# Two first blocks turned into token order in PSUM, constants and memory loads first, and value sums moved inside a unit

## The chip, the cores and the metric

The kernel runs on one core of a Trainium2 chip. Its five engines run their own instruction queues side by side: TensorE (PE, with PEld for its weight loads), VectorE (DVE), ScalarE (ACT), GpSimd (POOL) and SyncE (SP). SP, ACT and POOL also issue DMAs. The metric is the device time of one execution in microseconds, as the median of several runs. What the profile shows comes from one execution.

## The reference

A chunked attention with a memory, followed by a gated feed-forward layer. There are 4 sequences of 768 tokens with 8 heads of 64. Chunks are 32 tokens; each chunk sees 16 tokens to its left, 8 to its right and 8 memory rows of its sequence. The feed-forward layer takes the 3,072 tokens with 512 features each.

```python
for c in range(S // 32):
    l_start, r_end = max(0, 32 * c - 16), min(S, 32 * c + 32 + 8)
    k_full = concatenate([mem_k, k[:, :, l_start:r_end]], axis=2)
    v_full = concatenate([mem_v, v[:, :, l_start:r_end]], axis=2)
    scores = q[:, :, 32 * c:32 * c + 32] @ k_full.T / sqrt(64)
    a = exp(scores - max(scores)); a = a / sum(a)
    out[:, :, 32 * c:32 * c + 32] = a @ v_full
x = out.transpose(0, 2, 1, 3).reshape(3072, 512)
result = (maximum(x @ w_gate, 0) * (x @ w_val)) @ w_out
```

## The kernel before

The tokens are worked in 8 blocks (n = 0 to 7) of 384, two for each sequence. A block has 4 windows of 96 queries; a window's keys are 120 tokens and the 8 memory rows, which is 128 partitions. Heads are taken in 4 pairs (hp). All matmuls are F16 with F32 sums in PSUM. The program is written in its final order by hand (`manual_schedule`); each engine runs its queue in that order and waits on semaphores where data or a buffer is missing.

*Attention of one head pair* goes through steps:

- `step_s`: four score matmuls (one a window) of keys `kT` against `qbd`, which holds the pair's two heads of q beside zeros, so that one matmul of 192 columns does both heads; then the exponential on ScalarE into `ex`. In blocks 0 and 1 a mask matmul (`maskk`, `maskq`) starts each window's sum; later blocks mask by a bias in three exponentials.
- `step_v` (blocks 2 and up): eight matmuls of `ex` against `vwin`, which holds v beside 64 columns of ones, so that `x_ps` gets the weighted sum and the sum of the exponentials; then the logarithm on ScalarE. `step_e` makes the reciprocal by an exponential, `step_m` multiplies on VectorE into `xT`.
- `step_wide` (blocks 0 and 1): the same as sixteen matmuls of 64 output rows, first the eight that read only the ones, then the eight that read v, with logarithm, exponential and multiply behind them.

*Getting q and k turned.* Blocks 2 and up load k and q as tokens and turn them with DMA transposes (`turn_dma`, `spread_q`). Blocks 0 and 1 load four tokens to a partition row (J = 4, 1 KB pieces), cast them to F16 (`cast_k`, `cast_q`, which the program gives to an engine each) and turn them on TensorE (`turn_pe`): for each j of 4 a matmul against the selection matrix `sel` for k and a transpose against `ident` for q, into `k_ps` and `q_ps`, where the tokens lie j by j. `turn_copy` copies them to SBUF on VectorE: for k it puts the tokens in order, for q it keeps groups by j, and the scores of blocks 0 and 1 read `qbd` in steps instead.

*The feed-forward layer* is 12 units a block (m), each of four gate matmuls (`g_ps`), four value matmuls (`v_ps`), a relu on ScalarE (`gr`) and a product on VectorE (`gv`). Three output units a block take 12 matmuls each. `g_ps`, `v_ps`, `o_ps`, `k_ps`, `q_ps` and the fillers share four PSUM buffers. `fill` issues matmuls on zeros.

*Order.* Block 0's attention; four units' matmuls and block 1's attention; the other units of blocks 0 and 1 in turn; their output units, with block 2's steps between (`FIRST`). From there the units of block n run with the steps of block n + 1 after them: the table `AFTER` puts s, v and e of head pair hp after units 3hp, 3hp + 1 and 3hp + 2, and `AHEAD` puts m before unit 3hp + 3. `loads` issues a block's DMAs, most on POOL's queue; the memory rows go from HBM into `mem` once and from there by four small DMAs on SP's queue into `vwin` (`load_v_mem`).

## Time and profile before

| what | us |
|---|---|
| runs | 266.35, 266.36, 263.42 (median 266.35) |
| the profiled execution's own time | 266.13 |
| its span, first to last instruction | 264.4 |
| PE busy | 247.5 (94%), 1,660 matmuls |
| ACT busy | 143.2 (54%) |
| POOL busy | 107.3 (41%) |
| DVE busy | 103.4 (39%) |
| DMA, mean over the span | 110 GB/s, 29.00 MB |

The shares are averages over stages that differ. PE's includes fillers and matmuls at a low clock, so its 94% does not mean that the work would take that long at the full clock. A matmul's own duration is longer than the distance to the next one, because matmuls are pipelined; distances are read from starts, or from the chain of waits, which lists each step up to the start of the next.

### The profile page before, as it was taken

What the parts mean: (1) busy time and instruction counts of PE and PEld (TensorE: products, weight loads), DVE (VectorE), ACT (ScalarE), POOL (GpSimd) and SP (SyncE); (2) the same over time, 40 slices, a digit from 0 to 9 for tenths busy, and PEclk for the clock granted to TensorE, in tenths of its full rate; (3) what the DMA queues carried; (4) which work ended last, traced back from release to release, by engine and by line L of the source; (5) the groups of instructions that cost most, each with busy time, mean ns of one, the idle gap of its engine ahead of it and who ended that gap; (6) DMA issues with size and microseconds to landing.
All of it is one profiled execution on the core that took longest, in us unless ns stands there. A gap on an engine that the chain in (4) does not pass through costs nothing.

```text
span 264.4 us, 4462 instructions
## 1 busy us (share of the span) xinstructions
PE 247.5 (94%) x1660; PEld 140.2 (53%) x1660; DVE 103.4 (39%) x189; ACT 143.2 (54%) x268; POOL 107.3 (41%) x142
## 2 busy tenths in 40 slices
PE   6959669979999999999999999999999999999994
PEld 2535335546655455665566556655665466546641
DVE  6712573134443123555055504550456055604410
ACT  2224403443332797886388638863886388723311
POOL 7999743774729105049505940495031000000000
PEclk9977755699999999999999999999999999999999
DMA  7999999999999927949973995599670210021012
GB/s 173 199 154 175 207 203 196 144 145 131 162 101 65 146 81 83 145 77 96 181 136 65 105 182 116 75 92 166 136 84 0 82 41 0 2 79 40 2 40 79
DMA packets 114616, 29.00 MB, mean 110 GB/s; under 512 B 102339, under 2 KB 111523, under 8 KB 114595
## 3 DMA queue, kind: packets, MB, share of 16 engines
q0 software_dynamic: 84896, 14.74, 71.7%
q1 hardware_dynamic: 28866, 13.19, 23.2%
q10 hardware_dynamic: 832, 0.79, 1.1%
q8 instruction: 13, 0.21, 0.3%
q14 instruction: 9, 0.07, 0.1%
HBM read 31.15 MB, written 6.29 MB: 142 GB/s over the span
## 4 chain that ended last, share of the span: by engine, by line
PE 83%; ACT 5%; DMA 4%; DVE 3%; issue 2%; SPq 1%; POOL 1%; POOLq 0%; DVEq 0%
PE g_ps L312 23%; PE v_ps L312 23%; PE o_ps L330 21%; PE sc_ps L239 5%; PE x_ps L263 5%; DMA mem<-in_mem_v_dram 3%; PE idle L395 2%; PE sc_ps L236 1%; PE x_ps L289 1%; ACT ex L249 1%; DMA vwin<-mem 1%; ACT rinvw L295 1%; ACT ln L266 1%; DVE xT L296 1%; SPq L130 1%
## 5 line engine op out<-in xcount | busy, mean ns | idle before, releaser
L320 DVE TENSOR_TENSOR gv<-v_ps,gr 128x384 f16<-128x384 f32 x96 | 53.4, 558 | 98.1 <-PE v_ps L312 58.6
L312 PE MATMUL g_ps<-xT,wg 128*128 128x384 f16 x384 | 80.4, 327 | 2.2 <-DVE xT L296 2.1
L312 PE MATMUL v_ps<-xT,wv 128*128 128x384 f16 x384 | 80.4, 327 | 0.0
L330 PE MATMUL o_ps<-wo,gv 128*128 128x512 f16 x288 | 64.1, 379 | 0.0
L319 ACT ACTIVATE gr<-g_ps 128x384 f16<-128x384 f32 x96 | 46.9, 490 | 28.0 <-DVE gv L320 23.5
L312 PEld LDWEIGHTS <-wv 128*128 128x128 f16 x384 | 37.6, 98 | 27.2 <-issue 2.9
L312 PEld LDWEIGHTS <-wg 128*128 128x128 f16 x384 | 36.2, 98 | 20.6 <-issue 0.3
L330 PEld LDWEIGHTS <-gv 128*128 128x128 f16 x288 | 28.1, 98 | 32.0
L220 POOL COPY qbd<-qT 64x1536 f16<-64x1536 f16 x12 | 17.6, 1463 | 57.7 <-DMA qT<-q16n 57.3
L125 POOL DMA_DIRECT2D vwin<-in_v_dram x32 | 29.3, 939 | 19.7 <-PE x_ps L263 14.0
L333 ACT COPY o_sb<-o_ps 128x512 f32<-128x512 f32 x24 | 14.1, 587 | 40.3 <-PE o_ps L330 40.3
L278 DVE TENSOR_TENSOR xT<-x_ps,rinv 64x384 f16<-64x384 f32 x48 | 26.4, 550 | 20.0 <-ACT rinv L271 19.7
L249 ACT ACTIVATE ex<-sc_ps,bias 128x256 f16<-128x256 f32 x72 | 28.9, 472 | 8.7 <-PE sc_ps L239 8.7
L239 PE MATMUL sc_ps<-qbd,kT 128*128 128x192 f16 x128 | 26.4, 309 | 0.0
L125 POOL DMA_DIRECT2D k<-in_k_dram x24 | 21.5, 904 | 3.4 <-DMA wv<-in_moe_w_val_dram 1.7
L271 ACT ACTIVATE rinv<-ln,mln 64x768 f32<-64x768 f32 x24 | 22.2, 925 | 0.1
L266 ACT ACTIVATE ln<-x_ps 64x768 f32<-64x768 f32 x24 | 19.4, 807 | 5.0 <-PE x_ps L263 4.7
L146 POOL DMA_DIRECT2D q16n<-in_q_dram x24 | 18.7, 798 | 8.3 <-DMA wo<-in_moe_w_out_dram 5.7
L242 ACT ACTIVATE ex<-sc_ps 128x768 f16<-128x768 f32 x8 | 6.5, 811 | 25.1 <-PE sc_ps L239 25.1
L395 PE MATMUL idle<-filler 128*128 128x512 f16 x28 | 13.3, 606 | 4.6 <-DVE gv L320 3.3
L239 PEld LDWEIGHTS <-kT 128*128 128x128 f16 x128 | 12.3, 103 | 8.9 <-issue 6.1
L263 PEld LDWEIGHTS <-vwin 128*128 128x128 f16 x192 | 11.1, 97 | 8.2 <-issue 4.4
(64 smaller groups left out, 113.9 us busy)
## 6 DMA issues: line engine op xcount, KB each, us to landing
out_dram<-o_sb SPq DMA_DIRECT2D x24, 256.0 KB
vwin<-in_v_dram POOLq DMA_DIRECT2D x24, 120.0 KB, 6.0
q16n<-in_q_dram POOLq DMA_DIRECT2D x24, 96.0 KB, 4.3
k<-in_k_dram POOLq DMA_DIRECT2D x18, 120.0 KB, 4.1
wo<-in_moe_w_out_dram POOLq DMA_DIRECT2D x3, 512.0 KB, 17.3
wg<-in_moe_w_gate_dram POOLq DMA_DIRECT2D x2, 512.0 KB, 9.1
wv<-in_moe_w_val_dram POOLq DMA_DIRECT2D x2, 512.0 KB, 10.9
kst<-in_k_dram SPq DMA_DIRECT2D x4, 224.0 KB
```

The costliest lines, as they stand in the source:

```text
L125: pool_dma(dsts[p][m0:m1, i, :, 0:D], src)
L146: pool_dma(q16s[n][:, i], src)
L239: nc.tensor.matmul(s_out, lhsT=kT[:, i, hp, :], rhs=rhs, start=not rows, stop=True)
L249: nc.scalar.activation(dst, src, ACT.Exp, scale=SCALE, bias=bias[:, g:g + 1])
L263: nc.tensor.matmul(X[:, hh, QB * i:QB * i + QB], lhsT=vw[:, i, 2 * hp + hh, :], rhs=ex[:, i, hh, :], start=True, stop=True)
L266: nc.scalar.activation(ln, X[D:128, :, 0:TB], ACT.Ln, scale=1.0 / 64.0)
L271: nc.scalar.activation(rinv, lns.pop((n, hp)), ACT.Exp, scale=-1.0, bias=mln64[0:D, :])
L278: nc.vector.tensor_tensor(out=xT[D * hh:D * hh + D, hp, :], in0=X[0:D, hh, 0:TB], in1=rinv[:, hh, :], op=ALU.mult)
L312: nc.tensor.matmul(ps, lhsT=w[:, f, 128 * m:128 * m + 128], rhs=xTs[n][:, f, :], start=(f == 0), stop=(f == NFC - 1))
L319: nc.scalar.activation(gr, g_ps, ACT.Relu)
L320: nc.vector.tensor_tensor(out=gvs[n][:, m, :], in0=v_ps, in1=gr, op=ALU.mult)
L330: nc.tensor.matmul(o_ps, lhsT=gvs[n][:, m, 128 * t:128 * t + 128], rhs=wo[:, m, :], start=(m == 0), stop=(m == NDC - 1))
```

## The change

Five things change.

1. *Turning in PSUM.* `k_ps` and `q_ps` are in token order: the matmul for each j writes every fourth column. For q the transposes become plain matmuls, so `q_ps` is F32. The copies read PSUM in a row and write in a row, and the scores of blocks 0 and 1 read `qbd` in a row.
2. *Constants.* The ones of both `vwin` buffers are written as 32-bit words. All that clears and fills block 1's buffers moves from the middle of the first units to the start of the program: ones and edge rows on VectorE, the zeros of `qbd` on ScalarE as copies of the zero filler; the clearing of v's edge rows goes from POOL to VectorE. The second selection matrix is built on POOL ahead of the first weight loads.
3. *Memory first.* The memory rows of v are the first load on POOL's queue, and the four v loads of block 0 follow the constants `ident` and `sel`.
4. *Fillers.* Two more at the head, two before the last turn of block 0, two before its third `step_wide`, one in block 1.
5. *Value sums.* `ffn_unit` can run steps between its gate and its value matmuls; `step_v` of the steady loop moves from after unit 3hp + 1 to the middle of unit 3hp + 2. `x_ps` becomes one tile for the whole program.

```diff
     def turn_pe(n, hp):
-        kps = fps.tile([128, J, NQ, 32], F32, tag="f", name="k_ps")
-        qps = fps.tile([128, J, NQ, QR // NQ], F16, tag="f", name="q_ps")
+        kps = fps.tile([128, NQ, 128], F32, tag="f", name="k_ps")
+        qps = fps.tile([128, 512], F32, tag="f", name="q_ps")[:, 0:TB]
...
-            kj = kps[:, j].rearrange("p i t -> p (i t)")
+            kj = kps.rearrange("p i m -> p (i m)").rearrange("p (r j) -> p j r", j=J)[:, j]
...
-            qj = qps[:, j].rearrange("p i r -> p (i r)")
+            qj = qps.rearrange("p (r j) -> p j r", j=J)[:, j]
             if n == 0:
-                nc.tensor.transpose(qj, lq[:, hp, j].rearrange("p h d -> p (h d)"), ident[:QR, :QR])
+                nc.tensor.matmul(qj, lhsT=lq[:, hp, j].rearrange("p h d -> p (h d)"), rhs=ident[:QR, :QR],
+                                 start=True, stop=True)
...
     def turn_copy(n, hp):
-        dve_copy(kT_of(n)[:, :, hp, :].rearrange("p i (t j) -> p i t j", j=J), kps.rearrange("p j i t -> p i t j"))
+        dve_copy(kT_of(n)[:, :, hp, :], kps)
...
-            dve_copy(qbds[n][s, :, hp, hh, :].rearrange("p i (j r) -> p i j r", j=J),
-                     qps[s].rearrange("p j i r -> p i j r"))
+            dve_copy(qbds[n][s, :, hp, hh, :], qps[s].rearrange("p (i m) -> p i m", m=QB))
...
     def step_s(n, hp):
-            rhs = qb[:, i, hp]
+            rhs = qb[:, i, hp].rearrange("p h m -> p (h m)")
             if rows:
-                rhs = rhs.rearrange("p h (j r) -> p h r j", j=J)
...
-    def ffn_unit(n, m):
+    def ffn_unit(n, m, between=()):
         ffn_open(n, (m,))
-        ffn_mm(n, [(f, x) for x in range(2) for f in range(NFC)])
+        ffn_mm(n, [(f, 0) for f in range(NFC)])
+        for piece in between:
+            piece()
+        ffn_mm(n, [(f, 1) for f in range(NFC)])
         ffn_close(n)
...
-    nc.vector.memset(vwins[0].rearrange("p i h c -> p (i h) c")[:, :, D:128], 1.0)
+    def ones(p):
+        w = vwins[p].rearrange("p i h c -> p (i h c)").bitcast(U32).rearrange("p (a c) -> p a c", c=D)
+        nc.vector.memset(w[:, :, D // 2:D], 0x3C003C00)
+    ones(0)
...
+    ones(1)
+    nc.vector.memset(vwins[1][96:BAND, NQ - 1], 0.0)
+    w1 = vwins[1][96:112].rearrange("p i h c -> p (i h c)").bitcast(U32).rearrange("p (a c) -> p a c", c=D)
+    nc.vector.memset(w1[:, H * (NQ - 1):, D // 2:D], 0x3C003C00)
+    zero_qbd(1, lambda ap: nc.scalar.activation(
+        ap, bass.AP(tensor=filler.tensor, offset=filler[0:D].offset, ap=[[512, D], [0, NQ * HP], [1, QB]]), ACT.Copy))
...
-    zero_qbd(1, nc.vector.memset)
-    nc.vector.memset(vwins[1].rearrange("p i h c -> p (i h) c")[:, :, D:128], 1.0)
-    nc.vector.memset(vwins[1][96:BAND, NQ - 1, :, D:128], 0.0)
-    nc.vector.memset(vwins[1][96:112, NQ - 1, :, D:128], 1.0)
...
-        for d, w in enumerate("sve"):
-            AFTER[3 * hp + d] = [(w, hp)]
+        AFTER[3 * hp] = [("s", hp)]
+        WITHIN[3 * hp + 2] = [("v", hp)]
+        AFTER[3 * hp + 2] = [("e", hp)]
```

The start of POOL's queue before (`vwin_102` is block 0's v buffer, `mem` the memory rows, `sel_94` the first selection matrix):

```order
L125 DMA vwin_102<-in_v_dram 104x8x64
L370 MEMSET ident 128x128
L371 ISA
L371 AFFINE_SELECT ident<-ident 128x128
L358 MEMSET sel_94 128x128
L363 AFFINE_SELECT sel_94<-sel_94 128x4x30
L366 AFFINE_SELECT sel_94<-sel_94 128x4x2
L125 DMA vwin_102<-in_v_dram 120x8x64
L375 DMA mem<-in_mem_v_dram 8x32x64
L125 DMA vwin_102<-in_v_dram 120x8x64 x2
```

and after the change:

```order
L384 DMA mem<-in_mem_v_dram 8x32x64
L387 MEMSET ident 128x128
L388 ISA
L388 AFFINE_SELECT ident<-ident 128x128
L373 MEMSET sel_94 128x128
L378 AFFINE_SELECT sel_94<-sel_94 128x4x30
L381 AFFINE_SELECT sel_94<-sel_94 128x4x2
L127 DMA vwin_102<-in_v_dram 104x8x64
L127 DMA vwin_102<-in_v_dram 120x8x64 x3
```

The memory load has gone from behind two v loads to the head; the v loads stand behind the constants.

VectorE's queue before, from the last multiplies of block 0 to the first turn copies of block 1 (`qbd_99` and `vwin_103` are block 1's buffers):

```order
L296 TENSOR_TENSOR xT<-x_ps,rinvw 128x384 x3
L350 MEMSET qbd_99 64x16x48 x2
L454 MEMSET vwin_103 128x32x64
L455 MEMSET vwin_103 24x8x32
L456 MEMSET vwin_103 16x8x64
L320 TENSOR_TENSOR gv<-v_ps,gr 128x384 x2
L202 CAST kT<-k_ps 128x4x128
```

and VectorE's queue after, at its head, where those of `vwin_103` have gone:

```order
L347 MEMSET filler 128x256
L352 MEMSET vwin_102 128x32x32
L355 MEMSET vwin_102 16x512
L361 MEMSET qbd_98 64x16x48 x2
L362 MEMSET mln_111 128x1
L352 MEMSET vwin_103 128x32x32
L364 MEMSET vwin_103 24x512
L366 MEMSET vwin_103 16x8x32
L158 CAST lk_115<-kst 114x2x4x64
```

Three of the five memsets of block 1's buffers stand ahead of the first cast of k now; the two of `qbd_99` are on ScalarE's queue.

TensorE's queue at the first value sums of the steady loop, before (the eight sums are cut to the first and the last):

```order
L312 MATMUL v_ps<-xT,wv 128x384
L263 LDWEIGHTS vwin_103
L263 MATMUL x_ps<-ex,vwin_103 128x96
...
L263 MATMUL x_ps<-ex,vwin_103 128x96
L312 LDWEIGHTS wg
L312 MATMUL g_ps<-xT,wg 128x384
```

and after:

```order
L312 MATMUL g_ps<-xT,wg 128x384
L264 LDWEIGHTS vwin_103
L264 MATMUL x_ps<-ex,vwin_103 128x96
...
L264 MATMUL x_ps<-ex,vwin_103 128x96
L312 LDWEIGHTS wv
L312 MATMUL v_ps<-xT,wv 128x384
```

Before, the sums stand between one unit's value matmuls and the next unit's gate matmuls; now between the gate and the value matmuls of that next unit.

## The prediction

> **What bounds the kernel now.** I read the page first, then the windows by stage, then the chain of waits of the first 57 us, then the timeline where that chain leaves TensorE, and last the steady part of the loop. Each fence names its view.

> The page's first line, then three of the windows (length, busy time and count of PE, PEld, DVE, ACT, POOL; granted clock, DMA share, GB/s):

> ```profile
> span 264.4 us, 4462 instructions
> ```
> ```profile
> 25.60:36.60 11.00, 5.96 (x56) 3.00 (x54) 6.62 (x11) 3.53 (x7) 6.50 (x14) 0.71 1.30 206
> 36.60:57.00 20.40, 18.69 (x167) 10.41 (x167) 6.72 (x16) 7.54 (x13) 13.20 (x16) 0.65 1.69 171
> 57.00:83.00 26.00, 25.91 (x160) 15.48 (x159) 11.61 (x21) 10.17 (x21) 13.93 (x14) 1.00 1.64 116
> ```

> From 57 us on TensorE has no idle time to speak of and its full clock. Before that, in the first two blocks, it is idle for whole microseconds and granted 0.65 to 0.71 of its clock. The chain of waits (start, us, what) says what ends last there:

> ```profile
> 4.81 6.71 DMA mem<-in_mem_v_dram
> ...
> 13.91 3.56 DMA vwin<-mem
> ...
> 17.90 0.54 PE k_ps L185 x4
> 18.44 0.32 PE q_ps L194 x4
> 18.76 0.85 PE idle L395 x2
> 19.61 0.16 PE sc_ps L236
> 19.77 0.30 PE sc_ps L239
> ...
> 23.98 0.09 PE sc_ps L236
> 24.07 0.32 PE sc_ps L239
> ```

> The value sums of the first head pair wait for the memory rows, which are issued at 4.81, land at 11.52 and are then copied into four windows, the last at 17.47. The score rows show a second thing: a mask matmul of 192 columns takes 0.16 at the low clock and 0.09 at the full one, but the score matmul of the same width 0.30 to 0.32 at both. It reads its moving operand in steps of 24 elements, at 1.6 ns a column.

> Two pieces of the timeline, of TensorE and then of all engines, show the long stalls:

> ```profile
> 13.88 0.36 PE L289 MATMUL x_ps<-ex,vwin 128*64 128x96 f16 x8
> ...
> 17.61 0.29 PE L289 MATMUL x_ps<-ex,vwin 128*64 128x96 f16 x2 [0.69 <-DMA vwin<-mem]
> ```
> ```profile
> 30.12 0.70 DVE L350 MEMSET qbd<- 64x768 uint32 x1
> ...
> 34.50 0.48 DVE L456 MEMSET vwin<- 16x512 f16 x1 [0.17 <-DVE vwin L455]
> 35.02 1.02 DVE L320 TENSOR_TENSOR gv<-v_ps,gr 128x384 f16<-128x384 f32 x2
> 35.62 1.01 PE L395 MATMUL idle<-filler 128*128 128x512 f16 x2 [3.33 <-DVE gv L320]
> ```

> **The change part by part.** The sum runs against the profiled execution, 266.13 us (span 264.4 and 1.73 around it), 0.22 below the median of 266.35.

> *The start, -1.2* (a minus is time lost). VectorE ahead of its first cast, then ScalarE's first cast and one of its later copies by size:

> ```profile
> 1.59 1.76 DVE L345 MEMSET vwin<- 128x2048 f16 x1 [0.37 <-issue]
> ...
> 5.72 0.42 DVE L156 CAST lk<-kst 114x512 f16<-114x512 f32 x1
> ```
> ```profile
> 5.09 0.62 ACT L160 CAST lq<-qst 96x512 f16<-96x512 f32 x1 [3.00 <-DMA qst<-in_q_dram]
> ...
> 111.58 0.81 ACT L266 ACTIVATE ln<-x_ps 64x768 f32<-64x768 f32 x1 [0.21 <-PE x_ps L263]
> ```

> The ones become 1,024 words; at the 0.91 ns a word of L350 (768 in 0.70) that is 0.95, 0.81 less. Added are the second buffer's ones (0.95), a zero of 512 words (0.48, as L456), ones on 256 words (0.24) and two waits on itself of 0.17: 2.0. The first cast, and the first turn behind it, come 1.2 later (0.9 to 1.6). That covers two more fillers at the head, and ScalarE's new zeroing: two copies of 1,536 elements, 3.2 us at the 1.05 ns of L266 (768 in 0.81), nearly all of which fits into the 3.00 that ScalarE waits for q. Without the cover the zeroing would cost its 0.2 and the fillers 0.85.

> *Memory first, +3.2.* The eight value sums that read rows of v could follow the first eight at 14.24 and end at 14.6; they end at 17.9. The memory load moves from behind two of the v loads to the head of POOL's queue, at 1.4. If it takes 6.71 again it lands at 8.1, and the last copy, now 5.95 later, at 14.05, before the sums need it. The four v loads pass behind the constants, but POOL issues the same instructions ahead of the last of them as now. A rest of the stall may stay: 2 to 3.3.

> *Score steps, +5.2.* There are 8 steps of 4 pairs. A pair takes 0.46 at the low and 0.41 at the full clock and will take twice the mask's time, 0.32 or 0.18. All at the low clock that is 32 x 0.14 = 4.5, all at the full 32 x 0.23 = 7.4. Not all of it is path, since VectorE's copies come due next.

> *Turns, -1.5.* A head pair's turn writes 4 x 128 and 4 x 96 columns in 0.54 + 0.32. No row shows a stepped PSUM write. If free, it costs nothing more; if a column costs what the stepped read does, 896 x 1.57 = 1.41, 0.55 more, 4.4 over eight turns. A gain is excluded at an unchanged clock, for the columns are as many. I take a third: two of the eight turns lie beside a wait for VectorE, and the step is 4 elements, not 24. [...]

> *Copies, -1.2.* The copies out of PSUM now read in order, but q is F32:

> ```profile
> 6.85 0.69 DVE L202 CAST kT<-k_ps 128x512 f16<-128x512 f32 x1 [0.70 <-PE k_ps L185]
> 7.45 0.71 DVE L205 COPY qbd<-q_ps 64x384 f16<-64x384 f16 x2
> ```

> L202's 1.34 ns an element makes 0.52 of a q copy that is 0.35 now: 16 x 0.17 = 2.7 at most, none if the steps were what cost L202 its time. About half lies where scores wait for it.

> *Fillers, -1.3.* Five more on the path, 0.43 each at the low clock and half that at the full one: 1.1 to 2.1.

> *Memsets out of the middle, +3.3.* From 30.12 to 34.98 VectorE clears the second block's buffers, and the first products queue behind that; TensorE idles 3.33 for it. Next late are the products themselves and the first turn copy. On POOL the second selection matrix moves from behind block 1's v loads to ahead of the first weight loads: four instructions, which delay block 0's last two casts. The turn that needs them comes two score steps later, so that is hidden.

> *Clock, +5.0.* A mean of 0.65 in 36.6 to 57 is 14.3 us at half clock. 4.4 of that are stepped reads (14 x 0.31) that no clock shortens; half of the rest is 4.9. Between 17.9 and 23.98, where the mask shows the full clock again, five fillers (2.1), a turn (0.86) and the next sums (0.8) would save 1.8. That makes 0 to 6.7. I take 5.0: both long stalls go and fillers are added. [...]

> Front: -1.2 + 3.2 + 5.2 - 1.5 - 1.2 - 1.3 + 3.3 + 5.0 = 11.5.

> *Value sums between gate and value, +3.4.* One head pair of the steady loop on ScalarE, TensorE and VectorE, and a row of the waits from 103 to 240 (total, times):

> ```profile
> 109.79 1.20 ACT L249 ACTIVATE ex<-sc_ps,bias 128x256 f16<-128x256 f32 x3 [0.41 <-PE sc_ps L239]
> ```
> ```profile
> 110.23 0.81 PE L312 MATMUL v_ps<-xT,wv 128*128 128x384 f16 x4
> 111.04 0.50 PE L263 MATMUL x_ps<-ex,vwin 128*128 128x96 f16 x8
> 111.38 0.81 PE L312 MATMUL g_ps<-xT,wg 128*128 128x384 f16 x4
> ```
> ```profile
> 113.75 1.11 DVE L278 TENSOR_TENSOR xT<-x_ps,rinv 64x384 f16<-64x384 f32 x2 [0.25 <-ACT rinv L271]
> ```
> ```profile
> PEld L263 <- issue: 4.4, 20, 0.2
> ```

> The exponentials end at 110.99 and the sums start at 111.04. Four value matmuls move TensorE on by 0.65, so it was through at 110.88: 0.16 lost, twenty times, 3.2; the weight loads' own wait totals 4.4. With four gate matmuls ahead of them the sums find the exponentials done. Next late would be the multiply that frees x_ps, at 114.86; the next sums come at least three units of 1.3 after 111.38, not before 115.3, and both move by the same 0.5. Sum: 11.5 + 3.4 = 14.9, so 251.2.

> **The rivals.** A) Stepped writes cost as much as stepped reads, and with TensorE streaming less the clock rises late: turns -4.4 for -1.5, clock 1.5 for 5.0. The total is 8.5, 257.6 (254 to 260). For it: the only stepped row there is. Against: F32 in steps of 16 bytes is not F16 in steps of 48. [...]

> B) The front outruns the loads of block 2. On POOL and TensorE:

> ```profile
> 69.25 2.98 POOL L220 COPY qbd<-qT 64x1536 f16<-64x1536 f16 x2
> ```
> ```profile
> 86.10 0.49 PE L239 MATMUL sc_ps<-qbd,kT 128*128 128x192 f16 x4
> ```

> The block's q is spread by 72.2, in POOL's queue behind the loads of block 3, and first used at 86.1. More than 13.9 can't be gained ahead of it: 266.1 - 13.9 - 3.7 = 248.5, or 247 if that queue moves up.

> C) VectorE becomes the bound of the first blocks: start -1.6, copies -2.7, clock 1.5, and of the score steps only 2.0 count. Front -1.6 + 2.5 + 2.0 - 1.5 - 2.7 - 1.3 + 3.3 + 1.5 = 2.2, with 2.5 of the loop 4.7: 261.4, within 2%. For it: a head pair takes 0.69 + 1.04 + 0.5 of VectorE, against about 2.0 of TensorE at the full clock. Against: VectorE is busy 6.72 of 20.4 us now.

> D) Slower, by the stepped writes alone. Without their term the gain is 16.4. Over 7,168 columns that is gone at 2.3 ns more than the 0.96 of now, 3.3 ns a column, twice the stepped read; at 4.4 ns the turns cost 24.7 more and the time is 274.

> **How the numbers follow.** Forecast 48%, A 24%, B 10%, C 13%, D 5%. The time is the forecast's, 251.2. The range of 247 to 259 takes in B, the forecast's own bounds (248.5 to 254.5) and nearly all of A; it leaves out C, D and a little of A, 19%. Two per cent is 5.3 us, about what a measurement here tells from no change: below 261.0 lie the forecast, B, nearly all of A and a quarter of C, 84%; within 2% the rest of A and of C, 11%; slower D, 5%.

> **What would show it.** Right: the first value sums in one run without a DMA wait; no memset on VectorE after 10 us; score pairs of about 0.18; in the loop an x_ps group that starts as the gate group ends. Wrong: turn matmuls of 0.2 each (A, D); the first out-unit's scores waiting for POOL (B); scores that wait for the q copies in every head pair (C); a granted clock still below 0.7 beyond 30 us.

## The result and the profile after

The changed kernel takes 249.24 us (median of 248.6, 248.9, 249.57 and 249.59); the kernel before, beside it on the same chip, 264.88 (263.41 to 266.36). The ratio is 0.9406, 95% interval 0.9329 to 0.9484. The forecast was 251.2. The gain between these medians is 15.6; the 14.9 of the sum was taken from a single execution of 266.13, and from 264.88 it would have given 250.0.

The profiled execution took 249.59 us, 16.54 less than the one of before. The page of the profile, with its row of the granted clock and the first line of its chain:

```profile
span 247.9 us, 4445 instructions
...
PEclk9999999999999999999999999999999999999999
...
PE 65%; DMA 18%; POOL 9%; ACT 3%; issue 3%; POOLq 0%
```

The same three windows as of before, in which the changed kernel is further on in its work (length, busy time and count of PE, PEld, DVE, ACT, POOL; granted clock, DMA share, GB/s):

```profile
25.60:36.60 11.00, 10.63 (x141) 7.21 (x139) 8.53 (x16) 5.30 (x10) 7.33 (x15) 1.00 1.30 206
36.60:57.00 20.40, 18.52 (x138) 11.11 (x138) 7.98 (x15) 9.16 (x18) 12.21 (x15) 1.00 1.71 170
57.00:83.00 26.00, 23.61 (x147) 13.18 (x146) 7.33 (x14) 12.63 (x24) 14.29 (x15) 1.00 1.74 152
```

The clock is full in all of them, where it was 0.71 and 0.65. New is that TensorE has idle time in the third, where it had none. The timeline shows what it waits for, on TensorE and then on POOL:

```profile
73.21 0.49 PE L241 MATMUL sc_ps<-qbd,kT 128*128 128x192 f16 x4 [1.94 <-POOL qbd L225]
```
```profile
67.66 0.90 POOL L127 DMA_DIRECT2D vwin<-in_v_dram  x1 [2.89 <-PE v_ps L312]
69.29 0.84 POOL L127 DMA_DIRECT2D vwin<-in_v_dram  x1 [0.73 <-DMA k<-in_k_dram]
70.17 2.98 POOL L225 COPY qbd<-qT 64x1536 f16<-64x1536 f16 x2
```

Block 2's first scores come at 73.21, not at 86.10, and wait 1.94 for the spread of block 2's q, which stands in POOL's queue behind block 3's v loads and starts at 70.17 (69.25 before).

Four marks cut each span into pieces that can be compared: the end of the first head pair's value sums (the start of what TensorE does behind them), the first product on VectorE (block 0's attention lies ahead of it), the restart of the feed-forward units behind block 1's attention, and block 2's first scores. The times below are of the profiled executions; "wait" is the time for which the first scores wait for POOL. Two of e8's four runs, 250.50 and 250.56, the profiled one, are slow ones at a lower clock (mean over the span 0.976 and 0.984, for 1.000 and 0.992 of the others), and its median and ratio are of the other two.

| kernel | median us | first sums' end | first product | restart | first scores (wait) | from there to the end of the span |
|---|---|---|---|---|---|---|
| before | 264.88 | 17.83 | 35.02 | 57.51 | 86.10 | 178.3 |
| after | 249.24 | 15.43 | 26.00 | 42.52 | 73.21 (1.94) | 174.7 |
| e1 spread early | 247.21 | 13.79 | 24.35 | 40.86 | 70.94 (1.32) | 174.7 |
| e2 sums after the unit | 252.35 | 16.09 | 26.65 | 43.16 | 71.83 | 178.3 |
| e3 old turn | 251.11 | 15.58 | 27.43 | 46.33 | 76.21 | 174.7 |
| e4 memsets in the middle | 252.12 | 14.26 | 28.89 | 46.35 | 74.93 | 174.7 |
| e5 memory later | 250.96 | 17.54 | 28.10 | 44.62 | 73.20 | 174.7 |
| e6 old fillers | 248.74 | 15.35 | 25.48 | 41.78 | 73.97 (3.44) | 174.6 |
| e7 plain writes | 247.34 | 15.81 | 26.02 | 41.89 | 70.57 | 174.6 |
| e8 no fillers | 246.66 | 13.77 | 24.02 | 39.89 | 72.57 (3.93) | 176.2 |
| e9 four moved | 246.03 | 14.26 | 24.28 | 40.15 | 68.74 | 174.7 |
| e10 front undone | 260.10 | 18.07 | 35.24 | 55.20 | 83.79 | 174.7 |
| e11 stalls back | 256.99 | 17.76 | 34.59 | 52.23 | 80.81 | 174.7 |
| e12 no transposes | 262.06 | 17.50 | 34.68 | 57.77 | 86.36 | 174.6 |

So the change gains 15.0 up to the restart, gives 2.1 of it back up to the first scores (1.94 of it the wait), and gains 3.6 behind them.

How much of a difference is chance can be read from e1 and e2, whose edits lie behind the restart. Their first sums end at 13.79 and 16.09, 2.3 apart, with the same code as the changed kernel's 15.43. From there to the first product all three take 10.56 to 10.57, and from the product to the restart 16.51 to 16.52. So a difference of up to 2.3 at the first mark, or in a restart through it, says nothing by itself, while the two pieces behind it repeat to 0.01.

The loop first. One head pair on TensorE:

```profile
93.13 0.81 PE L312 MATMUL g_ps<-xT,wg 128*128 128x384 f16 x4
93.78 0.50 PE L264 MATMUL x_ps<-ex,vwin 128*128 128x96 f16 x8
94.12 0.81 PE L312 MATMUL v_ps<-xT,wv 128*128 128x384 f16 x4
```

Each group starts 0.65 or 0.34 behind the one ahead of it; the gap of 0.16 is gone. Then the start of VectorE's queue, with the first cast behind block 1's constants, and a turn and a score pair of TensorE at the full clock:

```profile
4.90 0.91 DVE L352 MEMSET vwin<- 128x1024 uint32 x1 [0.16 <-issue]
5.98 0.48 DVE L364 MEMSET vwin<- 24x512 uint32 x1 [0.17 <-DVE vwin L352]
6.58 0.27 DVE L366 MEMSET vwin<- 16x256 uint32 x1
6.88 0.72 DVE L158 CAST lk<-kst 114x512 f16<-114x512 f32 x1
...
8.92 1.11 DVE L211 CAST qbd<-q_ps 64x384 f16<-64x384 f32 x2
```
```profile
8.87 0.60 PE L190 MATMUL k_ps<-sel,lk 114*128 114x128 f16 x4
9.27 0.54 PE L199 MATMUL q_ps<-ident,lq 96*128 96x96 f16 x4
9.60 0.64 PE L408 MATMUL idle<-filler 128*128 128x512 f16 x2
10.07 0.25 PE L240 MATMUL sc_ps<-maskq,maskk 128*128 128x192 f16 x1
10.15 0.25 PE L241 MATMUL sc_ps<-qbd,kT 128*128 128x192 f16 x1
10.24 0.25 PE L240 MATMUL sc_ps<-maskq,maskk 128*128 128x192 f16 x1
...
12.96 0.64 PE L289 MATMUL x_ps<-ex,vwin 128*64 128x96 f16 x14
15.27 0.23 PE L289 MATMUL x_ps<-ex,vwin 128*64 128x96 f16 x2 [1.66 <-DMA vwin<-mem]
```

By starts, a turn takes 0.73 (8.87 to 9.60), a mask and score pair 0.17 (10.07 to 10.24), though each of its two matmuls is listed with 0.25. A q copy takes 0.55. Of the first sums only the last window's still wait for memory rows, 1.66.

### The profile page after: what moved, and what is told of

Read it like the earlier page. It is cut to its first block, busy times and chain, and to the rows that moved or that the text cites. A ratio compares the mean times of both kernels' runs of the same rounds, so it can differ in the third digit from the quotient of the medians.

```text
span 247.9 us, 4445 instructions
## 1 busy us (share of the span) xinstructions
PE 232.3 (94%) x1667; PEld 137.5 (55%) x1667; DVE 103.6 (42%) x187; ACT 144.2 (58%) x270; POOL 106.9 (43%) x141
## 4 chain that ended last, share of the span: by engine, by line
PE 65%; DMA 18%; POOL 9%; ACT 3%; issue 3%; POOLq 0%
PE o_ps L333 21%; PE g_ps L312 19%; PE v_ps L312 19%; DMA k<-in_k_dram 10%; DMA wg<-in_moe_w_gate_dram 6%; PE x_ps L264 3%; PE sc_ps L241 3%; DMA lk<-in_k_dram 3%; POOL vwin L127 2%; ACT ex L251 1%; POOL qbd L225 1%; ACT ln L267 1%; POOL k L127 1%; POOL wv L151 1%; ACT o_sb L336 0%
## 5 line engine op out<-in xcount | busy, mean ns | idle before, releaser
L320 DVE TENSOR_TENSOR gv<-v_ps,gr 128x384 f16<-128x384 f32 x96 | 53.4, 558 | 95.1 <-ACT gr L319 69.9
L312 PE MATMUL g_ps<-xT,wg 128*128 128x384 f16 x384 | 80.2, 326 | 2.2 <-DVE xT L296 2.1
L312 PE MATMUL v_ps<-xT,wv 128*128 128x384 f16 x384 | 80.0, 326 | 0.0
L312 PEld LDWEIGHTS <-wg 128*128 128x128 f16 x384 | 37.3, 98 | 23.1 <-issue 0.3
L312 PEld LDWEIGHTS <-wv 128*128 128x128 f16 x384 | 36.5, 98 | 24.5 <-issue 2.7
L127 POOL DMA_DIRECT2D vwin<-in_v_dram x32 | 28.8, 910 | 5.3 <-PE v_ps L312 3.9
L241 PE MATMUL sc_ps<-qbd,kT 128*128 128x192 f16 x128 | 17.8, 246 | 2.2 <-POOL qbd L225 1.9
L241 PEld LDWEIGHTS <-kT 128*128 128x128 f16 x128 | 11.6, 98 | 5.5 <-issue 2.2
L408 PE MATMUL idle<-filler 128*128 128x512 f16 x35 | 11.9, 457 | 1.3 <-DVE filler L347 1.3
```

Source lines behind the costliest of these rows:

```text
L127: pool_dma(dsts[p][m0:m1, i, :, 0:D], src)
L241: nc.tensor.matmul(s_out, lhsT=kT[:, i, hp, :], rhs=rhs, start=not rows, stop=True)
L312: nc.tensor.matmul(ps, lhsT=w[:, f, 128 * m:128 * m + 128], rhs=xTs[n][:, f, :], start=(f == 0), stop=(f == NFC - 1))
L320: nc.vector.tensor_tensor(out=gvs[n][:, m, :], in0=v_ps, in1=gr, op=ALU.mult)
```

## The experiments

The theory by this reading: the five parts gain each about what its stall or its matmuls cost, a full clock adds to it, and the loads of block 2 take 2 us back. The kernels were run in three groups, each beside the kernel before on its chip (medians 263.43 for e1 to e4, 265.19 for e5 to e8 and 264.75 for e9 to e12), so kernels of different groups are compared by their ratios.

**e1, the floor.**

```diff
-    loads(3)
+    load_band(3, k, k16s)
+    load_k_mem(3)
+    load_q_tokens(3)
+    spread_q(2, pool_copy)
+    load_band(3, v, vwins)
+    load_v_mem(3)
     turn_dma(3)
...
-    spread_q(2, pool_copy)
```

> The changed kernel with one step moved on POOL: block 2's q is spread between block 3's k and q loads and its v loads, not behind them all. Theory (the front outran the loads, and 1.94 us of what it gained is given back where block 2's first scores wait for POOL): the spread is done some 3 us earlier, the 1.94 wait goes, the time is 249.2 - 1.9 = 247.3. Rival (the DMA queues are the floor, POOL's copy only the last of them): the spread waits as long for the transposed q, or the next transfer is late by as much, and the time stays within 0.5 of 249.2.

247.21 us (246.49 to 248.08), ratio 0.9401 (0.9365 to 0.9437). TensorE and POOL:

```profile
70.94 0.49 PE L241 MATMUL sc_ps<-qbd,kT 128*128 128x192 f16 x4 [1.32 <-POOL qbd L225]
```
```profile
67.91 2.98 POOL L225 COPY qbd<-qT 64x1536 f16<-64x1536 f16 x2 [5.43 <-DMA qT<-q16n]
```

The time is the 247.3 of the theory, but against the kernel before, run beside each, e1's ratio is that of the changed kernel (0.9406), so the times show no gain. Nor did the wait go: it fell from 1.94 to 1.32, since POOL now waits 5.43 for the transposed q, and the restart was 1.66 earlier by chance. What the traces do show is that the floor lies apart from the front. In the eleven profiled executions with the old order on POOL, the kernel before among them, the spread starts between 68.79 and 70.94, though their restarts run from 39.9 to 57.8. With the spread moved ahead it starts at 67.91 here and at 67.54 in e7. So there are two floors: POOL's queue, and some 2 us ahead of it the transfers, as the rival had it.

**e2, the loop.** `step_v` goes back to its old place; `x_ps` stays one tile.

```diff
-        WITHIN[3 * hp + 2] = [("v", hp)]
+        AFTER[3 * hp + 1] = [("v", hp)]
```

> The changed kernel with the steady loop's value sums back after unit 3hp + 1; all else as changed, the single x_ps tile too. Theory (the loop's 3.6 us are twenty gaps of 0.16 to 0.27 in which the sums wait for the exponentials): the gaps come back and the time is 252.4 to 252.8. Rival (part of the loop's gain came from the single x_ps tile or from the loads having ended earlier): less than 2 of the 3.6 come back, under 251.2.

252.35 us (251.76 to 254.8), ratio 0.9613 (0.9557 to 0.9669). The span behind the first scores is 178.3, exactly that of before: all 3.6 is the place of the sums, nothing the tile. The waits from 103 to 230 have the weight loads' row again, which the changed kernel lacks:

```profile
PEld L264 <- issue: 3.8, 17, 0.2
```

Its front, the same code as the changed kernel's, differs by chance in two ways: the first scores did not wait (its spread started at 68.79), and TensorE kept half its pace until 13.6 (a mask and score pair 0.32 by starts), where the changed kernel had the full pace from its first turn at 7.66. The granted clock does not show that: its mean over the span is 0.998 in e2 and 1.000 in the changed kernel.

**e3, the turns.** `turn_pe`, `turn_copy` and the score reads of before: PSUM j by j, q by transposes into F16, scores that read `qbd` in steps.

```diff
-            kj = kps.rearrange("p i m -> p (i m)").rearrange("p (r j) -> p j r", j=J)[:, j]
+            kj = kps[:, j].rearrange("p i t -> p (i t)")
...
-                nc.tensor.matmul(qj, lhsT=lq[:, hp, j].rearrange("p h d -> p (h d)"), rhs=ident[:QR, :QR],
-                                 start=True, stop=True)
+                nc.tensor.transpose(qj, lq[:, hp, j].rearrange("p h d -> p (h d)"), ident[:QR, :QR])
...
+                rhs = rhs.rearrange("p h (j r) -> p h r j", j=J)
```

> The changed kernel with the turns, the copies and the score reads of before (q by transposes, PSUM j by j, scores that read in steps). Theory A (the clock is full because TensorE has no long stall): full clock as now; score pairs 0.41 for 0.165, 32 x 0.245 = 7.8 lost; turns 0.37 for 0.73, 8 x 0.36 = 2.9 gained; q copies 0.35 for 0.55, at most 16 x 0.2 = 3.2 gained, half of it on the path. The first units restart 3.3 later, at 45.8; 1.94 of that is hidden by the wait for POOL, so 250.6. [...]

251.11 us (250.59 to 252.57), ratio 0.9557 (0.951 to 0.9604). A turn and a pair at the full clock:

```profile
16.02 0.39 PE L189 MATMUL k_ps<-sel,lk 114*128 114x128 f16 x4
16.25 0.34 PE L198 MATMUL q_ps<-ident,lq 96*128 96x96 f16 x4
16.42 0.60 PE L410 MATMUL idle<-filler 128*128 128x512 f16 x2
16.86 0.24 PE L240 MATMUL sc_ps<-maskq,maskk 128*128 128x192 f16 x1
16.94 0.49 PE L243 MATMUL sc_ps<-qbd,kT 128*128 128x192 f16 x1
17.25 0.26 PE L240 MATMUL sc_ps<-maskq,maskk 128*128 128x192 f16 x1
```

A turn 0.40, a pair 0.39 to 0.41. The restart is 3.8 later, theory A's 3.3 and some low clock just ahead of it. The clock was full from 14 to 45 with five of the eight old turns in it, and low for one stretch of 3.4 at the head and one from 45.4 to 48.9, which costs another 1.3 behind the restart (by windows 0.91 from 6.2 to 26, 1.00 from 25.6 to 36.6, 0.92 from 36.6 to 57). So theory A's full clock did not quite hold, but the old turns alone do not bring the old clock back: from 26 to 54 it is 0.94 here and 0.63 in before. In the two pieces that repeat the old turns take 1.28 and 2.38 more (11.85 and 18.90), 3.7 in all.

**e4, the constants.** Block 1's memsets on VectorE behind `step_wide(0, 3)`, v's edge rows on POOL.

```diff
     step_wide(0, 3)
+    zero_qbd(1, lambda ap: nc.vector.memset(ap, 0.0))
+    nc.vector.memset(vwins[1].rearrange("p i h c -> p (i h) c")[:, :, D:128], 1.0)
+    nc.vector.memset(vwins[1][96:BAND, NQ - 1, :, D:128], 0.0)
+    nc.vector.memset(vwins[1][96:112, NQ - 1, :, D:128], 1.0)
```

> The changed kernel with what clears and fills block 1's buffers back in the middle of the first units, on VectorE (v's edge rows on POOL). Theory (the stall is worth its own length): VectorE's first cast comes 1.1 earlier, the first products 3.5 to 5 later; the units restart 2.5 to 4 later than 42.5, 1.94 of it hidden: 249.8 to 251.3, clock full but for a step. Rival (the stall was what pulled the clock down, and most of the 15 us came back with it): the granted clock falls below 0.75 between 30 and 50 as it did before, and the time is 254 or more.

252.12 us (251.28 to 253.16), ratio 0.9588 (0.9542 to 0.9634). The restart is 3.8 later. TensorE at the stall:

```profile
29.50 1.01 PE L402 MATMUL idle<-filler 128*128 128x512 f16 x2 [3.70 <-DVE gv L320]
30.44 1.06 PE L194 MATMUL k_ps<-sel,lk 114*64 114x128 f16 x8
31.21 0.93 PE L203 MATMUL q_ps<-ident,lq 96*64 96x96 f16 x8
```

From the first sums to the first product e4 takes 14.63, 4.06 more than the changed kernel, 3.70 of it in one wait: that is the stall. Behind its wait of 3.70 the k part of a turn takes 0.77 (30.44 to 31.21), twice the 0.41 of the same turn in the changed kernel; the clock is at half for one stretch, 3.4 us by its windows (0.990 over the whole span), and the piece up to the restart takes 17.46, 0.94 more. The truth lies between the two: the stall costs its length and one stretch of low clock, not the 20 us of before.

**e5, the memory rows.** POOL starts in the old order.

```diff
-    pool_dma(memv, bass.AP(tensor=mem_v.tensor, offset=mem_v[0, 0, 0, 0].offset,
-                           ap=[[D, NMEM], [NMEM * D, B * H], [1, D]]))
-    load_v_mem(0)
+    load_band(0, v, vwins, (0,))
...
-    load_band(0, v, vwins)
+    load_band(0, v, vwins, (1,))
+    pool_dma(memv, bass.AP(tensor=mem_v.tensor, offset=mem_v[0, 0, 0, 0].offset,
+                           ap=[[D, NMEM], [NMEM * D, B * H], [1, D]]))
+    load_v_mem(0)
+    load_band(0, v, vwins, (2, 3))
```

> The changed kernel with POOL's first loads in the old order: one v load, the constants, a v load, the memory rows, two v loads. Theory (moving the memory load was worth the sums' stall): the rows are issued near 4.8, not 1.4, land near 11.5 and are copied into the windows until 17.5; the first value sums end at 17.9, not 15.5; the units restart 2.4 later than 42.5, 1.94 of it hidden by the wait for block 2's q: 249.5 to 250.5, and the clock stays full. Rival (the long stall is what pulled the clock down before): the granted clock is below 0.8 between 14 and 26, the restart is 4 or more later, 252 or more.

250.96 us (249.59 to 253.09), ratio 0.9479 (0.9389 to 0.9568). The sums come in pieces, the last at 17.37, and the restart is 2.1 later:

```profile
14.30 0.36 PE L289 MATMUL x_ps<-ex,vwin 128*64 128x96 f16 x8
16.03 0.23 PE L289 MATMUL x_ps<-ex,vwin 128*64 128x96 f16 x2 [1.36 <-DMA vwin<-mem]
16.73 0.43 PE L289 MATMUL x_ps<-ex,vwin 128*64 128x96 f16 x4 [0.47 <-DMA vwin<-mem]
17.37 0.23 PE L289 MATMUL x_ps<-ex,vwin 128*64 128x96 f16 x2 [0.21 <-DMA vwin<-mem]
```

The clock from 14 to 26 was full, as the theory has it: a mask and score pair takes 0.16 by starts from 13.55 and from 19.18 on, and 0.32 from 11.19. But its interval and the changed kernel's overlap, and 2.1 in one restart is within the chance of the first mark. What the rows' place is worth shows in all the profiles together: in the nine with the rows first the first sums wait 0 to 1.7 for them and end at 13.8 to 16.1, in the five with the rows later (before, e5, e10, e11, e12) they wait 2.0 to 3.5 and end at 17.5 to 18.1, wherever the first turn began.

**e6 and e8, the fillers.** e6 has the counts of before, e8 none but the ten at the head.

```diff
-    fill(10)
+    fill(8)
...
-    fill(2)
     turn_pe(0, 3)
...
```

> The changed kernel with the old counts of fillers: eight at the head for ten, none before block 0's last turn and before its third value step, two for three in block 1. Theory A (denser real work keeps the clock up; the fillers cost only themselves, 5 x 0.235 = 1.2): the granted clock is as full as in the changed kernel, the restart is 0 to 1.2 earlier than 42.5, and behind the wait for block 2's q the time is the same, 248.5 to 249.5. Rival B (those five carry the clock): the granted clock is below 0.8 in a stretch of 4 us or more before 42, the restart is 2 or more later and the time is 250.5 or more.

> The changed kernel with no filler but the ten at the head. Theory A (the real work alone holds the clock): the granted clock stays above 0.95 from 8 us on, the restart is up to 3.5 earlier than 42.5 (some 15 fillers of 0.235), and the time is 248.5 to 249.5, for block 2's q is not ready earlier. Rival B (the fillers hold the clock): the granted clock falls below 0.8 for 4 us or more in one or more places between 8 and 42, which costs about half of each such stretch; the restart is between 42 and 47 and the time 249.5 to 253.

e6: 248.74 us (246.99 to 250.34), ratio 0.9366 (0.9279 to 0.9453). e8: 246.05 and 247.26, ratio 0.9309 (0.9204 to 0.9414). The windows of TensorE's clock from 6.2 to 26 and from 26 to 54 in e8:

```profile
6.20:26.00 19.80, 14.74 (x177) 11.81 (x178) 12.64 (x24) 9.68 (x17) 18.29 (x33) 0.91 1.60 162
26.00:54.00 28.00, 24.05 (x230) 15.76 (x230) 14.53 (x27) 13.49 (x25) 15.42 (x25) 1.00 1.52 187
```

0.91 of 19.8 is 3.6 us at half clock, a stretch between 6 and 14 that e3, e5 and e7 with all fillers have too; behind it the clock is full up to the first scores. (Theory A's "above 0.95 from 8 us on" missed that stretch.) e6 restarts 0.7 earlier, which the two pieces that repeat confirm (10.13 and 16.30, 0.66 less), e8 2.6, and in these executions both pay it back at the floor, waiting 3.44 and 3.93 for POOL. So theory A on the clock: the fillers do not carry it. That they cost nothing in the time is not shown: both ratios lie a little below the changed kernel's 0.9406, with overlapping intervals.

**e7, the stepped write.** On top of e1, the turns write PSUM in a row. The ordering is left out.

```diff
-            kj = kps.rearrange("p i m -> p (i m)").rearrange("p (r j) -> p j r", j=J)[:, j]
+            kj = kps.rearrange("p i m -> p (i m)")[:, 128 * j:128 * j + 128]
...
-            qj = qps.rearrange("p (r j) -> p j r", j=J)[:, j]
+            qj = qps[:, QR * j:QR * j + QR]
```

> The kernel with the spread of block 2's q moved ahead (247.2) and with turns that write PSUM in a row, j by j; copies and score reads as in the changed kernel, so the tokens of blocks 0 and 1 stay in the order in which j puts them and their results are not the reference's: the ordering is left out, nothing else. Theory (a stepped write costs 0.83 ns a column at the full clock, twice a plain one): a turn falls from 0.73 to 0.37 and the eight save 2.9 of TensorE, of which those beside a wait for VectorE's copies save nothing: restart 1.5 to 2.9 earlier than 40.9, and the time 246 to 247 as block 2's loads hold the rest back. Rival A (PSUM writes in steps cost nothing, the weights loaded for each j set the 0.73): the turns stay at 0.7. Rival C (VectorE's copies are the bound): turns of 0.37, restart within 0.5 of 40.9.

247.34 us (246.94 to 249.72), ratio 0.9354 (0.9274 to 0.9433), with e1's 247.21 no difference. A turn and the waits of TensorE for q copies:

```profile
11.46 0.39 PE L190 MATMUL k_ps<-sel,lk 114*128 114x128 f16 x4
11.69 0.34 PE L199 MATMUL q_ps<-ident,lq 96*128 96x96 f16 x4
11.86 0.60 PE L408 MATMUL idle<-filler 128*128 128x512 f16 x2
```
```profile
PE sc_ps L241 <- DVE qbd L211: 1.0, 2, 0.7
```

0.40 for 0.73: the step costs 0.33 a turn, 0.45 ns a column becomes 0.8. Rival A is out. From the first product to the restart e7 takes 15.87 and e1 16.51, 0.64 less where four turns save 1.3: VectorE's copies hold the other half, as the 1.0 of waits says. e8 and e9, which keep the stepped writes and leave out the fillers, take 15.87 there too, so the copies and exponentials are the next limit of this piece, only 0.65 below the changed kernel's 16.52. The forecast of a restart 1.5 to 2.9 earlier failed: the head of e7 had the low clock (0.91 from 6.2 to 26) and 1.7 of waits for memory rows, where e1's had none (0.999 over its whole span), and its restart came 1.0 later.

**e9, a better order.** e1, and three more moves:

```diff
-    for a in range(0, NDC, 4):
-        pool_dma(wo[:, a:a + 4, :], wo_src[:, a:a + 4, :])
...
-    loads(2)
+    load_band(2, k, k16s)
+    load_k_mem(2)
+    load_q_tokens(2)
     turn_dma(2)
+    for a in range(0, NDC, 4):
+        pool_dma(wo[:, a:a + 4, :], wo_src[:, a:a + 4, :])
+    load_band(2, v, vwins)
+    load_v_mem(2)
...
```

with no fillers behind the head, and `ones(1)` and the edge rows behind `turn_copy(0, 2)`.

> The changed kernel with four things together: block 2's q spread ahead of block 3's v loads; the three loads of the output weights moved behind block 2's k and q loads; no filler but the ten at the head; block 1's ones, zeros and edge rows on VectorE behind block 0's third turn copy instead of at the start. Theory (after the spread, the floor is the transfers of block 2's k and q, which wait for lanes behind the output weights; with those out of the way the front's gain comes through): restart of the units near 38.5, block 2's first scores 28.75 later at 67.3 without a wait, and 174.7 and 1.7 behind that: 243.6. Rival A (all loads together set the floor, whatever their order): first scores at 70 or later, 246 or more. Rival B (the output weights come late): output matmuls wait for a DMA near 65, 246 or more.

246.03 us (245.12 to 246.85), ratio 0.9306 (0.9238 to 0.9374). POOL and TensorE:

```profile
63.41 2.98 POOL L225 COPY qbd<-qT 64x1536 f16<-64x1536 f16 x2
```
```profile
68.74 0.49 PE L241 MATMUL sc_ps<-qbd,kT 128*128 128x192 f16 x4
```

The floor is gone: q is spread at 66.4 and the scores don't wait, nor do the output matmuls. But the restart is at 40.15, not 38.5, and the time 2.4 above the forecast. The first turn came 1.8 earlier (5.87), and met the next waits of the front: 1.2 for POOL's mask, 1.3 for the memory rows, 2.5 for q copies. It has the lowest median here, and all its runs lie below the changed kernel's, but its interval reaches the changed kernel's and that of e1.

**e10, e11 and e12, the clock.** e11 is e4 and e5 together; e10 adds e3's old turns (the fillers, the value sums and the early second selection matrix stay as changed); e12 is e10 with q turned by plain matmuls into F32, and asks whether the transposes hold the clock down.

```diff
-                nc.tensor.transpose(qj, lq[:, hp, j].rearrange("p h d -> p (h d)"), ident[:QR, :QR])
+                nc.tensor.matmul(qj, lhsT=lq[:, hp, j].rearrange("p h d -> p (h d)"), rhs=ident[:QR, :QR],
+                                 start=True, stop=True)
```

> The changed kernel with the old turns, block 1's memsets in the middle and the memory rows later, all at once; of the change the fillers and the value sums between gate and value stay. One alone left the clock up. Theory (the two stalls and the thinner score steps pull the clock down only together, as in the kernel before): the granted clock falls below 0.75 between 30 and 50, the restart is near 56, the time 260 to 263. Rival (with the new fillers the clock stays up): granted clock above 0.9 from 26 to 50, restart 42.5 + 3.8 + 3.8 + 2.1 = 52.2, first scores at 81, and 174.7 and 1.7 behind them: 257.4.

> The changed kernel with block 1's memsets in the middle and the memory rows later; the turns, copies and score reads stay as changed. Theory (both stalls together, without the thin score steps, do not hold the clock down): granted clock above 0.9 from 26 to 50, restart 42.5 + 3.8 + 2.1 = 48.4, first scores at 77.2, time 253.6. Rival (the stalls alone do it): granted clock below 0.75 between 30 and 50 and 256 or more.

> As the run with the front undone (old turns j by j, score reads in steps, memsets in the middle, memory later), but q turned by plain matmuls into F32 and not by transposes. [...]

e10: 260.1 us (259.86 to 260.69), ratio 0.9842 (0.9774 to 0.9911). e11: 256.99 (256.07 to 258.31), 0.9725 (0.9651 to 0.9799). e12: 262.06 (259.74 to 262.94), 0.989 (0.9845 to 0.9934). The window from 26 to 54 of before, then of e11, e10 and e12, with the clock third from the end:

```profile
26.00:54.00 28.00, 22.57 (x192) 12.09 (x191) 12.57 (x24) 9.54 (x17) 16.30 (x26) 0.63 1.56 185
```
```profile
26.00:54.00 28.00, 20.69 (x227) 13.11 (x226) 16.17 (x28) 11.40 (x21) 15.26 (x25) 0.94 1.52 185
```
```profile
26.00:54.00 28.00, 21.10 (x220) 11.29 (x215) 13.09 (x25) 10.49 (x19) 16.29 (x26) 0.88 1.56 188
```
```profile
26.00:54.00 28.00, 22.39 (x192) 11.94 (x191) 14.01 (x24) 9.08 (x16) 15.80 (x26) 0.70 1.57 187
```

With both stalls and the new turns (e11) the clock is low for 3.4 us ((1 - 0.94) x 28 x 2), with the old turns (e10) for 6.7, with old turns and no transposes (e12) for 16.8, before for 20.7. The theory of e11 was right on this window and wrong in the time, 3.4 too low; the time is the rival's 256 or more. With the early start the first sums waited 3.51 in one piece for the memory rows (its row names another DMA; the copies of the rows into the windows end at 17.4), and TensorE was at half clock from 15.8 to 22.7 as well (0.979 over the whole span). e10 comes out at the lower edge of its theory in time and nearer to the rival in clock. e12 gives no sign that the transposes hold the clock down: without them it was lower, 0.70 for 0.88, and the restart 2.6 later.

## Why the prediction was right

The time lies in the range, 2 us below the forecast; 1.2 of them come from the execution that the sum started from. In the sum of the steps the loop came out within 0.2, the front 3.5 above, and rival B took 2.1 back; the rival had a chance of 10%, and it came on top of the forecast, not in its place. That the floor took back most of what the front gained over its forecast is luck: the sum had no term for either.

The front's 15.0 can be cut at the marks: 2.4 up to the end of the first sums (17.83 to 15.43), 6.6 from there to the first product (17.19 to 10.57), 6.0 up to the restart (22.49 to 16.52).

- *Start and memory first, -1.2 + 3.2 = 2.0.* 2.4, and 2.8 between the means of the five profiles with the rows later and the nine with the rows first. The first cast moved from 5.72 to 6.88, 1.16; the first turn by 1.46, to 7.66. But only part of that was path: e9's first turn was 1.8 earlier and met waits for masks and rows. The rest of the stall that was allowed for is there, 1.66, and varies: e1 has none.
- *Turns, copies and score steps, -1.5 - 1.2 + 5.2 = 2.5.* 3.7 by e3. Score pairs fell from 0.41 to 0.17, so the 0.18 was right. The stepped write costs 0.33 a turn, 2.6 in all. By e7 the five turns behind the first sums cost 1.0 of their 1.7 on the path (10.57 to 10.21, and 16.51 to 15.87), so an estimate for all eight is 1.6, close to the term's 1.5, with another working. In e2, at the low clock, a turn takes 1.40 for the 0.73 of e7's first one, which is what rival A's 1.41 had; but the turns ran at the full clock, and the price follows the clock, which the stepped read does not (0.41 and 0.46). Rivals A and D are out. The factor is 1.8 to 1.9 (0.73 for 0.40, 1.40 for 0.73). The q copy takes 0.55 for 0.35, as the 0.52 said. Rival C is there in small: TensorE waits for the copies (1.0 in e7, 2.5 in e9), but behind the fillers they bound nothing.
- *Fillers, -1.3.* 0.7 by e6. That they were needed for the clock, which the term of the clock had among its reasons, is wrong.
- *Memsets, +3.3.* 4.1 by e4, with the stretch of low clock behind it left to the clock.
- *Clock, +5.0.* What the others leave of the pieces behind the first sums: 6.62 - 1.28 - 4.06 + 0.44 = 1.72 and 5.97 - 2.38 + 0.22 = 3.81 (turns and memsets taken off, fillers put back), together 5.5, within the 0 to 6.7. That this is the clock is argued, not shown by a run of its own, and it assumes that the other costs add. What speaks for it is the second piece. The windows from the first product to the restart, of before and of e10:

```profile
35.02:57.51 22.49, 20.08 (x169) 10.68 (x169) 8.31 (x19) 8.05 (x14) 13.77 (x17) 0.65 1.70 173
35.24:55.20 19.96, 17.55 (x170) 9.08 (x170) 8.32 (x19) 7.88 (x14) 11.41 (x14) 0.85 1.81 177
```

Low for 15.7 us ((1 - 0.65) x 22.49 x 2), it costs the 3.8 in before; low for 6.0, it costs 1.1 in e10 against e3's 18.90; low for 3.5, it costs 0.9 in e4 and 1.1 in e11 against the changed kernel's 16.52. That is 0.2 to 0.3 for each us of low clock in all four. The reason given for 5.0, that the fillers help, fell. The other, that both long stalls go, is not enough by itself: in before the low clock begins ahead of the stall of 3.33, while TensorE is still busy (windows of before, with the clock third from the end):

```profile
28.00:30.00 2.00, 1.01 (x16) 0.52 (x10) 0.54 (x1) 1.11 (x2) 0.83 (x2) 1.00 1.24 208
30.50:32.00 1.50, 1.50 (x17) 0.81 (x17) 1.01 (x2) 0.97 (x2) 1.29 (x5) 0.50 1.24 206
```

- *The sum of the front.* No term was off by more than 1.2, but all five lay low (0.4, 1.2, 0.6, 0.8 and 0.5), which makes the 3.5. Undone singly, turns, memsets, memory and fillers move the restart by 3.8 + 3.8 + 2.1 - 0.7 = 9.0. Of the 6.0 that this leaves, 1.4 lies ahead of the first sums' end, where chance makes up to 2.3 and where e4's earlier start is worth nothing if the sums wait for late memory rows. The other 4.6 is, by this reading, the part of the clock that no single one brings back.
- *Rival B.* The queue did not move up: the spread started at 70.17. The gain ahead of the first scores was 12.9, about the bound of 13.9 less the 0.9 by which it was later; by the spreads of the other executions that bound varies by 2. The forecast's front of 11.5 lay just below that floor, and a point 2.4 under a floor of 13.9 should have made its price part of the sum.
- *Value sums, +3.4.* 3.6, all of it by e2.

What is open: what starts the low clock, and why it lasts 3.4 us in one kernel and 17 to 21 in others. The long ones (before, e12) have score steps that read in steps and a stall of 3.3 to 3.9, but so has e10, with 6.7. e12's ten runs spread from 259.74 to 262.94; whether chance or q's turn sets the length is not settled.

## What to carry to other kernels

Cut a span at marks that all versions share, and learn from two executions of the same code which pieces vary: here the head did by 2.3, and the pieces behind it by 0.01. Read a front's gain at its last mark: several parts taken together gained 15.0 where their single costs sum to 9.0, and the place where the next block's loads arrive took 2.1 back. Ask for each gain which transfer is late next, and move that issue in the same change. Fillers that are there to keep the clock up may do nothing for it (in e8, with none but the ten at the head, the clock is 1.00 from 26 to 54, as with them); take them out once and measure.
